# Late weights in small pieces that wait for attention products, a first projection by pieces, and a new instruction order

## The chip, the cores and the metric

The kernel runs on one core of one Trainium2 chip. The metric is the device time of one execution in microseconds (us); lower is better. Before the change it was 254.84 us (median of three runs, 253.96 to 255.41). A change under 2% counts as "same".

Four engines and a queue matter here: TensorE (PE; PEld is its weight load), VectorE (DVE), ScalarE (ACT), GpSimd (POOL), and SyncE (SP), which issues nearly all transfers, in order.

All runs told below are of the state called fast, but for one run of the kernel before (259.79 us), which the ratios leave out. Within that state, the mean clock that TensorE was granted still takes three values, about 1.0, 0.993 and 0.987, and that turns out to matter; it is given where it does.

## The reference

One block of a transformer with adaptive normalisation: modulation from a condition vector, attention over 8 dilated neighbours, and a gated feed-forward layer. S = 2048 rows (16 tiles of 128), D = 512, F = 1792 (14 hidden blocks of 128), 32 heads of 16.

```python
mod = (_silu(c) @ w_mod).reshape(1, 6, 1, -1)
sa, ca, ga, sb, cb, gb = ...                      # shift, scale, gate, twice
h = _layernorm(x) * (1 + ca) + sa
x = x + ga * _A_ref(h, A_wqkv, A_wo)              # attention: key and value rows s, s-2, ..., s-14
h = _layernorm(x) * (1 + cb) + sb
x = x + gb * _B_ref(h, B_w1, B_w3, B_w2)          # (silu(h @ w1) * (h @ w3)) @ w2
```

## The kernel before

The program is a list of operations with their dependences. A list scheduler, driven by a table of one number per operation, decides the order on each engine and which buffer each value gets; semaphore waits follow from that. So the table of numbers is part of the kernel.

The loads and what late loads wait for:

```python
LATE = {"wms1": 0, "wmg1": 2, "w13_0": 0, "w13_1": 1, "w13_2": 1, "w13_3": 2, "w2": 2}
...
p.dma(x_sb[:, 0:2, :], ...)                       # x of tiles 0, 1
p.dma(wm_s[0][:], wm_view[:, :, 0:1024], ...)     # shift and scale, 1 MB
p.dma(x_sb[:, 2:4, :], ...)
for i in range(3):                                # q, k, v thirds, 0.52 MB each
    p.dma(wqkv[:, :, i * D:(i + 1) * D], ...)
...
p.dma(wm_g[0][:], wm_view[:, :, 1024:1536], ...)  # first gate, 0.52 MB
...
for g in range(NG):                               # w1 and w3 by groups of hidden blocks
    late[f"w13_{g}"] = [p.dma(w1[:, :, a:b], ...), p.dma(w3[:, :, a:b], ...)]
late["w2"] = [p.dma(w2[:], w2_view, ...)]         # all of w2, 1.8 MB
...
for name, T in LATE.items():
    for o in late[name]:
        o.deps[prods[T]] = True                   # waits for attention product q*k of tile T
```

The table of numbers, and not this text, sets the order in which SyncE sends them: x of tiles 0 and 1, the first modulation's weights, x of tiles 2 and 3, the gate, x of tiles 12 to 15, v's and k's thirds, x of tiles 4 to 11, and q's third last.

The first h (normalised, modulated and transposed x of tiles 0 and 1) is written in four pieces by ScalarE and VectorE, and a projection product waits for all of it:

```python
def mm(e, ft=ft, vp=vp):
    for t in range(KT):
        ins = e.matmul(bank(vp)[:, 0:n], wqkv[:, t, col:col + P], vh.at[:, t, 0:n], start=(t == 0), stop=(t == KT - 1))
p.op("pe", mm, 4 * c_mm(n), k, r=[vh, vwq[kind]] + qkv_hold, w=[vp])
```

For each tile of rows VectorE makes one attention product q*k (`sb_pq`, 2.3 us) and one of attention by values (`sb_vsh`), and TensorE sums each with narrow products against 0/1 matrices. v goes out to memory and comes back shifted.

The last two tiles make their output in two halves of columns, each over all 14 hidden blocks at once:

```python
if T >= NT - 2:
    for q in range(2):
        def mm(e, q=q, vz=Val("ps_z", psum)):
            for fi in range(NF):
                ins = e.matmul(bank(vz)[:, 0:n], vhh[fi].at[:, tt * P:(tt + 1) * P], w2[:, fi, q * n:(q + 1) * n], ...)
        p.op("pe", mm, 7 * MM, ("z", 2 * T + q), r=vhh + [vw2s], w=[vz])
```

The softmax here doesn't subtract the row's maximum and nothing guards it: scores larger than these inputs give would overflow.

## Time and profile before

| | before |
|---|---|
| timed runs | 254.84 us median of 3 |
| span of the profiled execution | 253.0 us |
| TensorE / VectorE / ScalarE busy | 243.6 (96%) / 186.8 (74%) / 121.6 us (48%) |
| granted clock | 1.000 |

The prediction below shows the lines. In short: TensorE is full from 25 us to the end, so the kernel can only fill it earlier, take out the small stands in the full stretch, or end sooner.

How to read: in a timeline line the columns are start and length in us, engine, source line, operation, output from inputs, shapes and count; the bracket is the idle time just before it and what ended it. In a list of waits they are the engine and line that waited, what for, then us in total, times and longest. In a busy table each digit is the busy share of one fortieth of the span in tenths.

I also use one sum of my own, the *slip*: the start of a run of products on TensorE, less where it would start if the run before it took its count times the durations that the prediction derives (0.2158 us for 512 columns and so on). A slip is a stand, or a slow clock, or the drain of a pipeline.

### The profile page before, as it was taken

How to read it: one execution, taken by the hardware profiler on the slowest of the kernel's cores; microseconds unless marked ns; L12 is line 12 of the kernel's file. 1: busy time of each engine (PE TensorE's matmuls, PEld its weight loads, DVE VectorE, ACT ScalarE, POOL GpSimd, SP SyncE). 2: the span in 40 equal slices, each digit the busy share in tenths (PEclk: the TensorE clock that was granted, in tenths of full speed). 3: DMA queues.
4: the chain of work that ended last, by engine and by line, in shares of the span. 5: the costliest groups of instructions: out<-in, count | busy, mean ns of one | idle time of the engine just before them, and what ended most of it. 6: DMA issues, size and time to landing. Idle time of an engine off the chain costs nothing.

```text
span 253.0 us, 5719 instructions
## 1 busy us (share of the span) xinstructions
PE 243.6 (96%) x2413; PEld 146.9 (58%) x2413; DVE 186.8 (74%) x289; ACT 121.6 (48%) x214; POOL 18.5 (7%) x48
## 2 busy tenths in 40 slices
PE   7787999999999999999999999999999999999995
PEld 6666557665567766546655554455544444447774
DVE  4869599999998999999998898958714334623432
ACT  2376886845696357722561452333651332332320
POOL 4133100000000020000000200004100000100000
PEclk9999999999999999999999999999999999999999
DMA  6995999998598992270278373275122000021001
GB/s 228 354 327 155 288 336 252 341 323 213 139 254 207 295 273 66 57 173 25 89 190 231 55 208 64 42 191 143 26 60 83 1 3 0 0 62 44 21 3 41
DMA packets 48817, 37.09 MB, mean 147 GB/s; under 512 B 22152, under 2 KB 39576, under 8 KB 48792
## 3 DMA queue, kind: packets, MB, share of 16 engines
q1 hardware_dynamic: 48784, 36.73, 52.6%
q8 instruction: 19, 0.31, 0.5%
q14 instruction: 6, 0.05, 0.1%
q10 hardware_dynamic: 8, 0.00, 0.0%
HBM read 30.67 MB, written 5.26 MB: 142 GB/s over the span
## 4 chain that ended last, share of the span: by engine, by line
PE 85%; DMA 6%; SPq 4%; DVE 1%; ACT 1%; issue 0%; DVEq 0%
PE pall L847 36%; PE pall L883 17%; PE pall L691 9%; PE pall L831 5%; PE pall L818 5%; DMA sb_wqkv<-in_A_wqkv_dram 5%; PE pall L749 5%; SPq L135 4%; PE pall L709 4%; PE pall L870 2%; PE pall L650 2%; DMA sb_al<-a_scratch_dram 2%; DVE sb_vsh L809 1%; ACT sb_xn L611 1%; PE pall L535 0%
## 5 line engine op out<-in xcount | busy, mean ns | idle before, releaser
L847 PE MATMUL pall<-sb_h,sb_w 128*128 128x512 bf16 (+1 forms) x560 | 101.4, 336 | 0.0
L847 PEld LDWEIGHTS pall<-sb_h,sb_w 128*128 128x128 bf16 x560 | 53.6, 98 | 40.9 <-ACT sb_h L658 0.2
L853 ACT ACTIVATE sb_sg<-pall 128x512 bf16<-128x512 f32 (+1 forms) x70 | 35.3, 511 | 65.6 <-PE pall L847 65.6
L856 DVE TENSOR_TENSOR sb_hh<-sb_sg,pall 128x512 bf16<-128x512 bf16 (+1 forms) x70 | 38.8, 575 | 25.2 <-PE pall L847 24.6
L883 PE MATMUL pall<-sb_w,sb_hh 128*128 128x512 bf16 x196 | 43.9, 379 | 0.0
L740 DVE TENSOR_TENSOR sb_pq<-sb_q,sb_kT 128x4096 bf16<-128x4096 bf16 x16 | 36.2, 2284 | 3.6 <-ACT sb_q L698 3.2
L691 PE MATMUL pall<-sb_h,sb_wqkv 128*128 128x512 bf16 (+1 forms) x160 | 31.1, 336 | 2.5 <-DMA sb_wqkv<-in_A_wqkv_dram 2.5
L883 PEld LDWEIGHTS pall<-sb_w,sb_hh 128*128 128x128 bf16 x196 | 18.9, 98 | 21.8
L893 DVE TENSOR_TENSOR sb_o<-pall,sb_x 128x512 bf16<-128x512 f32 (+1 forms) x18 | 11.2, 629 | 22.7 <-PE pall L883 17.6
L592 DVE BATCH_NORM_STATS2 sb_st<-sb_x 128x6 f32<-128x512 bf16 x32 | 21.8, 681 | 4.6 <-DMA sb_x<-in_A_x_dram 4.3
L809 DVE TENSOR_TENSOR sb_vsh<-sb_vsh,sb_al 128x4096 bf16<-128x4096 bf16 x10 | 22.9, 2286 | 1.0 <-DMA sb_al<-a_scratch_dram 0.9
L691 PEld LDWEIGHTS pall<-sb_h,sb_wqkv 128*128 128x128 bf16 x160 | 14.6, 97 | 12.6 <-issue 2.0
L598 POOL TENSOR_TENSOR sb_rs<-sb_mv,sb_cst 128x2 f32<-128x2 f32 x16 | 5.3, 330 | 198.2 <-DVE sb_mv L593 151.9
L658 ACT ACTIVATE sb_h<-pall,sb_modc 128x512 bf16<-128x512 bf16 (+1 forms) x30 | 18.9, 707 | 1.7 <-PE pall L650 1.5
L611 ACT ACTIVATE sb_xn<-sb_x,sb_nb,sb_rs 128x512 bf16<-128x512 bf16 x16 | 12.1, 806 | 10.6 <-DVE sb_nb L605 10.5
L749 PEld LDWEIGHTS pall<-sb_E,sb_pq 128*128 128x128 bf16 x512 | 14.8, 96 | 3.2 <-DVE sb_pq L740 0.5
L709 PE MATMUL pall<-sb_wqkv,sb_h 128*128 128x512 bf16 x64 | 16.0, 378 | 0.3 <-DMA sb_wqkv<-in_A_wqkv_dram 0.3
L831 PE MATMUL pall<-sb_wo,sb_ot 128*128 128x512 bf16 x64 | 16.3, 379 | 0.0
L824 ACT ACTIVATE sb_ot<-pall 128x512 bf16<-128x512 f32 x16 | 9.5, 595 | 12.5 <-PE pall L818 12.5
L749 PE MATMUL pall<-sb_E,sb_pq 128*128 128x32 bf16 x512 | 15.1, 176 | 0.3 <-DVE sb_pq L740 0.3
L809 DVE TENSOR_TENSOR sb_vshx<-sb_vshx,sb_al 128x4096 bf16<-128x4096 bf16 x6 | 13.7, 2283 | 0.0
L698 ACT ACTIVATE sb_q<-pall 128x512 bf16<-128x512 f32 (+1 forms) x20 | 10.0, 517 | 5.8 <-PE pall L691 5.6
(70 smaller groups left out, 192.3 us busy)
## 6 DMA issues: line engine op xcount, KB each, us to landing
sb_vsh<-v_scratch_dram SPq DMA_DIRECT2D x40, 256.0 KB, 4.6
sb_vshx<-v_scratch_dram SPq DMA_DIRECT2D x24, 256.0 KB, 4.3
sb_wm_s<-in_w_mod_dram SPq DMA_DIRECT2D x2, 1024.0 KB, 6.4
v_scratch_dram<-sb_v SPq DMA_DIRECT2D x16, 128.0 KB, 3.9
sb_w<-in_B_w_dram SPq DMA_DIRECT2D x4, 512.0 KB, 4.6
sb_w<-in_B_w_dram SPq DMA_DIRECT2D x1, 1792.0 KB, 11.8
out_dram<-sb_o SPq DMA_DIRECT2D x14, 128.0 KB, 1.7
sb_x<-in_A_x_dram SPq DMA_DIRECT2D x3, 512.0 KB, 10.5
```

What stands on the lines that cost most here:

```text
L592: o = p.op("dve", lambda e, m=m, T=T: e.bn_stats(st[:, m, :], x_sb[:, T, :]), 670, ("st", m), r=[vx[T]], w=[vs])
L658: return e.activation(vh.at[:, ft, 0:n * P], b[:, j * 512:j * 512 + n * P], ACT.Identity, bias=modc[:, 8 * which + ft:8 * which + ft + 1], ...
L691: ins = e.matmul(bank(vp)[:, 0:n], wqkv[:, t, col:col + P], vh.at[:, t, 0:n], start=(t == 0), stop=(t == KT - 1))
L709: ins = e.matmul(bank(vp), vh.at[:, t, tt * P:(tt + 1) * P], wqkv[:, t, 2 * D:3 * D], start=(t == 0), stop=(t == KT - 1))
L740: return e.tensor_tensor(vp.at[:], in0, in1, ALU.mult)
L749: ins = e.matmul(b[:, c0:c0 + H], vp.at[:, w, ft, :], E_sb[:, ft, :], start=(ft == 0), stop=(ft == KT - 1))
L809: return e.tensor_tensor(v_w, v_w, a_w, ALU.mult)
L831: ins = e.matmul(bank(vy), vt.at[:, ft, :], wo[:, ft, :], start=(ft == 0), stop=(ft == KT - 1))
L847: ins = e.matmul(bank(vp)[:, 0:n], wt[:, t, fi * P:(fi + 1) * P], vh.at[:, t, 0:n], start=(t == 0), stop=(t == KT - 1))
L853: p.op("act", lambda e: e.activation(vt.at[:, 0:n], bank(vgp)[:, 0:n], ACT.Silu), c_act(n), k, r=[vgp], w=[vt], table="silu")
L856: p.op("dve", lambda e: e.tensor_tensor(vh_.at[:, 0:n], vt.at[:, 0:n], bank(vup)[:, 0:n], ALU.mult), c_dve(n), k, r=[vt, vup], w=[vh_])
L883: ins = e.matmul(bank(vz), vhh[fi].at[:, tt * P:(tt + 1) * P], w2[:, fi, :], start=(fi == 0), stop=(fi == NF - 1))
```

## The change

The intent: get the projections' weights in sooner by letting the gate wait; let the first q products start on the first piece of h; spread the late weights, in pieces, behind chosen attention products; end without waiting for the last hidden block; and find a new order for all of it by searching from many seeds. The diff, cut:

```diff
-LATE = {"wms1": 0, "wmg1": 2, "w13_0": 0, "w13_1": 1, "w13_2": 1, "w13_3": 2, "w2": 2}
+LATE = [("wmg0", -1), ("wms1", 1), ("wms1b", 2), ("wmg1", -1), ("w1_0", 3), ("w3_0", 12), ("w1_1", 3), ("w3_1", -1), ("w1_2",
+        0), ("w3_2", 5), ("w1_3", 5), ("w3_3", 4), ("w2_0", 4), ("w2_1", 8), ("w2_2", 0), ("w2_3", 16)]
...
-    late["wms1"] = [p.dma(wm_s[1][:], wm_view[:, :, 1536:2560], ("load", 12), 1048576, w=[vwms[1]])]
+    for name, a, i in (("wms1", 0, 12), ("wms1b", 512, 26)):
+        late[name] = p.dma(wm_s[1][:, :, a:a + 512], wm_view[:, :, 1536 + a:2048 + a], ("load", i), 524288, part=[vwms[1]])
...
-        late[f"w13_{g}"] = [
-            p.dma(w1[:, :, a:b], w1_view[:, :, a:b], ("load", 14 + g), 4 * 128 * (b - a) * 2, part=[vw13[g]]),
-            p.dma(w3[:, :, a:b], w3_view[:, :, a:b], ("load", 14 + g), 4 * 128 * (b - a) * 2, part=[vw13[g]]),
-        ]
+        late[f"w1_{g}"] = p.dma(w1[:, :, a:b], w1_view[:, :, a:b], ("load", 14 + 2 * g), 1024 * (b - a), w=[vw1[g]])
+        late[f"w3_{g}"] = p.dma(w3[:, :, a:b], w3_view[:, :, a:b], ("load", 15 + 2 * g), 1024 * (b - a), w=[vw3[g]])
...
-    late["w2"] = [p.dma(w2[:], w2_view, ("load", 18), 1835008, w=[vw2])]
+    for g in range(NG):
+        late[f"w2_{g}"] = p.dma(w2[:, a:b, :], w2_view[:, a:b, :], ("load", 22 + g), 131072 * (b - a), w=[vw2[g]])
...
+    ORDER = (2, 0, 3, 1)
+    def proj(mm, n, k, vh, vp, vw):          # the first h: one product per piece, each waits for its own
...
+        for t in ORDER:
+            o = p.op("pe", lambda e, t=t: mm(e, (t,)), c_mm(n), k, r=[vh.pieces[t], vw] + qkv_hold, part=[vp], hold=[vh],
+                     after=[o] if o else [])
...
-                p.op("pe", mm, 7 * MM, ("z", 2 * T + q), r=vhh + [vw2s], w=[vz])
+                for a, c in ((0, 10), (10, NF)):
...
+                    o = p.op("pe", mm, (c - a) * c_mm(n), ("z", 2 * T + q), r=vhh[a:c] + ..., part=[vz], after=[o] if o else [])
...
-    for name, T in LATE.items():
-        for o in late[name]:
-            o.deps[prods[T]] = True
+    for name, n in LATE:                     # even n: product q*k, odd n: attention by values, of tile n // 2
+        if n >= 0:
+            late[name].deps[(prods, avs)[n % 2][n // 2]] = True
...                                           # and the whole table of priorities is new
```

Also changed, and not shown: the modulation's result passes two VectorE operations instead of three, w2 is scaled in four pieces instead of two, and there are 104 warm-up products (products of ones that nobody reads) instead of 80.

## The prediction

> **What bounds the kernel now.** I read the busy shares first, then the 40 slices, then the chain that ended last for what one product of each shape costs, then PE's timeline where the slices are not full.
>
> ```profile
> span 253.0 us, 5719 instructions
> PE 243.6 (96%) x2413; PEld 146.9 (58%) x2413; DVE 186.8 (74%) x289; ACT 121.6 (48%) x214; POOL 18.5 (7%) x48
> ...
> PE   7787999999999999999999999999999999999995
> DVE  4869599999998999999998898958714334623432
> DMA  6995999998598992270278373275122000021001
> ```
>
> PE is full from the fifth slice (25 us) to the last. A change of order cannot shorten that stretch much; it can only make PE full earlier, or end it sooner. So I split the span into products that must be made and the rest. The chain gives start, length and count of back-to-back runs:
>
> ```profile
> 95.44 0.45 PE pall L650 x8
> 97.84 0.79 PE pall L749 x32
> 193.28 20.72 PE pall L847 x96
> 235.63 7.87 PE pall L847 x72
> ```
>
> One 512-column product takes 20.72/96 = 0.2158 us, one of 256 columns 7.87/72 = 0.1093, one of 16 or 32 columns 0.79/32 = 0.0247, a transpose 0.45/8 = 0.056. With the counts of the groups by shape: 756 of 512 columns, 163.1 us; 344 of 256, 37.6; 1024 of 16 or 32, 25.3; 104 transposes, 5.8; modulation and gates (96 one-column products and 8 spreads), about 2.8. Sum 234.6 us; the 80 warm-up products are not in it. From the last product to the end are 2.65 us (250.38 to 253.03). So 253.0 - 234.6 - 2.65 = 15.7 us are neither work nor end. The timeline of PE shows where:
>
> ```profile
> 6.83 0.94 PE L535 MATMUL pall<-sb_csT_bf,sb_wm_s 128*128 128x1 bf16 x32 [0.42 <-DMA sb_wm_s<-in_w_mod_dram]
> ...
> 8.98 0.55 PE L567 MATMUL pall<-sb_csT_bf,sb_wm_g 128*128 128x1 bf16 x16 [0.52 <-DMA sb_wm_g<-in_w_mod_dram]
> ...
> 12.09 1.02 PE L709 MATMUL pall<-sb_wqkv,sb_h 128*128 128x512 bf16 x4 [0.33 <-DMA sb_wqkv<-in_A_wqkv_dram]
> ...
> 14.87 2.36 PE L691 MATMUL pall<-sb_h,sb_wqkv 128*128 128x256 bf16 x20 [0.78 <-DMA sb_wqkv<-in_A_wqkv_dram]
> ...
> 21.14 1.91 PE L691 MATMUL pall<-sb_h,sb_wqkv 128*128 128x256 bf16 x16 [1.74 <-DMA sb_wqkv<-in_A_wqkv_dram]
> ...
> 72.60 0.96 PE L749 MATMUL pall<-sb_E,sb_pq 128*128 128x32 bf16 x32 [0.29 <-DVE sb_pq L740]
> ...
> 82.59 0.96 PE L818 MATMUL pall<-sb_ind,sb_vsh 128*128 128x16 bf16 x32 [0.23 <-DVE sb_vsh L809]
> ...
> 244.07 6.29 PE L870 MATMUL pall<-sb_w,sb_hh 128*128 128x256 bf16 x56 [0.59 <-DVE sb_hh L856]
> ```
>
> The three thirds of wqkv arrive one after another at 12, 15 and 21 us, and each time PE stands until then. By 21.14 us PE has done about 8.3 us of the work above, so 12.8 of the 15.7 us lie before. Laying the runs end to end at the durations above, starts slip behind by another 2.6 us after 26 us: 0.73 ahead of L870, and some 1.9 in small pieces, most at L749 and L818, which wait for VectorE's attention products between 50 and 90 us.
>
> VectorE is the second limit there: 9 tenths from 30 to 100 us. It gets its first attention product late:
>
> ```profile
> 28.58 2.29 DVE L740 TENSOR_TENSOR sb_pq<-sb_q,sb_kT 128x4096 bf16<-128x4096 bf16 x1 [3.15 <-ACT sb_q L698]
> ```
>
> It idled 3.15 us, because q needs the third of wqkv that lands at 21.
>
> **The Trainium skill.** "TensorE: Matmul & The Clock Gate", section "Back-to-back issue gap", gives N/2.4 + 2.5 ns for a warm product: 109.2 and 215.8 ns for 256 and 512 columns. The trace agrees (0.1093, 0.2158). The page's 131 ns for a sustained stream at 512 is not seen here, so nothing faster is to be hoped for. "Perfetto Trace Analysis", section "Identifying the Most-Contended Engine", says that matmul busy time is a poor measure; hence pitches and not the 96%. "DMA: Bandwidth & Descriptors", section "Where 436 GB/s comes from", puts memory's share of one core at about 358 GB/s; one-microsecond stretches of this trace move 345 to 355 GB/s from 7 to 17 us. So the head is bound by bytes, and the order of loads decides. The same page, "Queues, rings and completion order", says that each ring starts descriptors in order; the wqkv landings in order of issue agree.
>
> **The change part by part.** The lists of instructions of the two kernels show what moved; the products that must be made are the same, so the 234.6 us stay.
>
> *Head.* Before, the queue holds x of two tiles, the first half of modulation weights, x of two tiles, the gate's 0.52 MB, x, two thirds of wqkv, 1 MB of x, then the last third. After: x, modulation, wq, x, x, wk, wv, then 1 MB of x; the gate's weights come behind. Bytes issued ahead decide the landing, so I take it from the load in the same place before. wk closes 3.15 MB, where before the first wqkv third landed at 12.0; wv closes 3.67 MB, where the second landed at 14.85; wq closes 1.84 MB, between x of tiles 2 and 3 (7.44) and the gate's weights (8.96): 8.2. The first modulation still waits for its load until 6.83. Its result passes two VectorE operations of 0.15 us instead of three, and these no longer stand behind two statistics (they began at 9.09 and ended at 10.0; I get 8.0). The pieces of the first h come at 8.6 to 9.4, and since each product takes its own piece, the first q products run from 8.75. Then 24 warm-up products (1.3 us, harmless, as wk is not there), q and a first k, wk at 12.0 with 8 products to 12.95, transposes of h1 to 13.4 (its normalised tiles come at 12.9, after four statistics of 0.82 us that wait for x at 8.96 and 10.5), 4 products to 13.85, then a wait for wv to 14.95. From there the list runs on: 8 v (1.73), 8 k or q (0.87), 4 v (0.86), 12 more (1.31), 16 transposes (0.9), 19 products (2.08), 4 v (0.86): the first product on h2 at 23.6 us. Before, it began at 25.74 + 4 x 0.216 = 26.6, but with 0.6 us of gate and 0.22 of transposes done that now come later. Gain 26.6 - 23.6 - 0.8 = 2.2 us.
>
> *Middle.* The rest of PE's list sums to 221.7 us at these pitches, so its last product would end at 245.3. VectorE's first attention product moves to about 25.5 us; it then waits for the gate's product (PE's place 28.4, so to 29.5) and runs 1.3 us behind its own sum. Setting its sums against PE's, the attention products stand ready 0.65 to 1 us ahead of PE up to 55 us and 1.5 or more afterwards, where before they were level or up to 0.7 us late. So of the 1.9 us of small slips I expect 0.9 to stay; gain 1.0 with the 0.22 us of warm-up products that before stood at 70.5. The small pieces of w1, w3 and w2 total the same bytes; their waits spread them, and their reward is that the attention's round trip through memory meets fewer of them. w2's scaling, in four pieces instead of two, costs some 0.15 us more on VectorE, which has that much.
>
> *End.* The last two tiles' products take the first 10 hidden blocks, then the last 4, so nothing waits for the last block: the 0.59 us wait (0.73 with its drain) goes. The end after the last product stays 2.65 us.
>
> Sum: 2.2 + 1.0 + 0.7 = 3.9 us; the other way, 245.3 + 0.2 drain + 0.9 slips + 2.65 = 249.0. Span 249.1. The timed median is 1.8 us above the profiled span (254.84 against 253.0): 250.9, rounded to **250.8 us**, 1.6% faster.
>
> **The rivals.** *All waste goes:* if wv lands by bandwidth alone (3.67 MB/350 GB/s + 2.9 = 13.4) PE saves another 1 us, and with no slips 0.9 more: 248.9. For it: slack is everywhere positive. Against it: the second third of wqkv, in the same place, took until 14.85. *A new wait replaces the old one:* VectorE now has to make all 16 statistics before its first product, and a load that waits for an attention product blocks the in-order SyncE queue behind it, v and attention loads included. That would make PE stand for VectorE between 30 and 60 us: 252 to 254. For it: the ahead-times there are under 1 us; w3's second piece goes out before wo. Against: between 45 and 50 us, when the first attention rows return, few weights are in flight. *The head is hidden anyway*, PE running dry later and waiting for h3 and h4 until about 26: 253. Against: transposes of h3 are due only at 26 us, with their tiles made by 24.
>
> **Range and chances.** Errors: 1 us at wv's landing, 0.9 on slips, up to 2 to the bad side from the queue. Eight in ten: 249.0 to 252.8. Faster by 2% needs 249.74, 1.1 us better than my sum: 0.20. Slower by 2%: 0.01. Within: 0.79.
>
> **What would show it.** PE's first q product near 8.8 us, waits for wk to 12 and wv to 15, first 512-column product on h2 near 23.6; VectorE's first attention product near 25.5; no wait ahead of the last 256-column products; fewer and smaller waits at attention products. Wrong if wv lands two microseconds off, if PE shows waits for attention products of over 1 us in sum, or if a queue wait for a product delays a load PE then waits for.

## The result, and the profile after

Four runs of the changed kernel took 250.60 to 251.69 us, median 251.06; four of the kernel before, 253.96 to 255.41, median 254.54. The ratio is 0.9862, with a 95% interval of 0.9822 to 0.9902: 1.4% faster, "same" by the 2% line. (A ratio is the mean time of one kernel's fast runs over that of the other's of the same rounds, so it is not quite the ratio of the medians.) The spans of the two profiled executions are 253.0 and 248.6 us.

The head of the page after, with busy times and the busy table:

```profile
span 248.6 us, 5772 instructions
PE 243.5 (98%) x2437; PEld 149.2 (60%) x2437; DVE 186.8 (75%) x289; ACT 123.3 (50%) x216; POOL 21.3 (9%) x48
...
PE   8989999999999999999999999999999999999995
DVE  3869799999898999999899897898942344232442
DMA  6999969679979993336779270436032000001001
```

Busy times of TensorE and VectorE are what they were. The span is 4.4 us shorter: TensorE is full from the fourth slice (19 us) instead of the fifth (25 us). All of TensorE's waits that the trace after shows:

```profile
PE pall L702 <- DMA sb_wqkv<-in_A_wqkv_dram: 1.4, 1, 1.4
PE pall L551 <- DVE sb_ones L448: 1.1, 1, 1.1
```

Before there were nine such rows. The second is the wait for the first instruction of all, as before. The first is a wait for k's third of the projection weights. From TensorE's timeline after, the lines that answer to those of before:

```profile
7.00 0.94 PE L535 MATMUL pall<-sb_csT_bf,sb_wm_s 128*128 128x1 bf16 x32
...
8.77 0.75 PE L702 MATMUL pall<-sb_h,sb_wqkv 128*128 128x256 bf16 x3
...
13.55 1.03 PE L702 MATMUL pall<-sb_h,sb_wqkv 128*128 128x256 bf16 x8 [1.36 <-DMA sb_wqkv<-in_A_wqkv_dram]
...
15.30 1.89 PE L721 MATMUL pall<-sb_wqkv,sb_h 128*128 128x512 bf16 x8
...
23.91 2.75 PE L702 MATMUL pall<-sb_h,sb_wqkv 128*128 128x512 bf16 x12
...
239.75 6.28 PE L885 MATMUL pall<-sb_w,sb_hh 128*128 128x256 bf16 x56
```

The first q product starts at 8.77. k's third makes TensorE stand until 13.55; v's third makes it stand no more (no bracket at 15.30). The first 512-column product on the third h is at 23.91, against 26.6 before. The last products start with no bracket. VectorE's timeline after:

```profile
25.88 2.29 DVE L752 TENSOR_TENSOR sb_pq<-sb_q,sb_kT 128x4096 bf16<-128x4096 bf16 x1 [0.45 <-ACT sb_kT L711]
...
29.25 0.16 DVE L571 CAST sb_gcol<-pall 128x4 bf16<-128x4 f32 x1 [0.76 <-PE pall L565]
...
29.73 2.28 DVE L752 TENSOR_TENSOR sb_pq<-sb_q,sb_kT 128x4096 bf16<-128x4096 bf16 x1
```

The first attention product starts 2.7 us sooner than before (28.58), after an idle time of 0.45 instead of 3.15 us; then VectorE waits for the gate's product, which now comes late.

Summed over the trace, slips are 9.8 us before and 4.2 after; that is 5.6 us less for a span 4.4 us shorter, as the 24 more warm-up products take 1.3 us. After 26 us they fall from 2.6 us (of which 0.73 ahead of the last products) and 0.22 us of warm-up products to about 0.25.

### The profile page after: what moved, and what is told of

It reads as the page before. It is cut to its first block, busy times and chain, and to the rows that moved or that the text cites. A ratio compares the mean times of both kernels' runs of the same rounds, so it can differ in the third digit from the quotient of the medians.

```text
span 248.6 us, 5772 instructions
## 1 busy us (share of the span) xinstructions
PE 243.5 (98%) x2437; PEld 149.2 (60%) x2437; DVE 186.8 (75%) x289; ACT 123.3 (50%) x216; POOL 21.3 (9%) x48
## 4 chain that ended last, share of the span: by engine, by line
PE 94%; DMA 4%; SPq 1%; issue 0%; DVE 0%
PE pall L859 39%; PE pall L897 17%; PE pall L702 11%; PE pall L843 6%; PE pall L721 6%; PE pall L761 5%; PE pall L830 5%; DMA sb_wqkv<-in_A_wqkv_dram 4%; PE pall L885 2%; PE pall L649 2%; SPq L135 1%; PE pall L535 0%; PE pall L565 0%; PE pall L575 0%; DVE sb_o L907 0%
## 5 line engine op out<-in xcount | busy, mean ns | idle before, releaser
L897 PE MATMUL pall<-sb_w,sb_hh 128*128 128x512 bf16 x196 | 44.4, 379 | 0.0
L821 DVE TENSOR_TENSOR sb_vsh<-sb_vsh,sb_al 128x4096 bf16<-128x4096 bf16 x12 | 27.2, 2283 | 0.4 <-DMA sb_al<-a_scratch_dram 0.2
L843 PE MATMUL pall<-sb_wo,sb_ot 128*128 128x512 bf16 x64 | 15.8, 378 | 0.0
L598 POOL TENSOR_TENSOR sb_rs<-sb_rs,sb_cst 128x2 f32<-128x2 f32 x16 | 13.9, 871 | 1.3
```

Of the source, the lines that this page charges most:

```text
L821: return e.tensor_tensor(v_w, v_w, a_w, ALU.mult)
L843: ins = e.matmul(bank(vy), vt.at[:, ft, :], wo[:, ft, :], start=(ft == 0), stop=(ft == KT - 1))
L897: ins = e.matmul(bank(vz), vhh[fi].at[:, tt * P:(tt + 1) * P], w2[:, fi, :], start=(fi == 0), stop=(fi == NF - 1))
```

## The experiments

Twelve kernels ran, two of them controls, in three calls: the first two on chip 5, the third on chip 15. Edits to order were made on the finished lists of each engine, so that nothing else moved; `sp`, `dve`, `pe` and `pool` are those lists and `key(...)` finds an operation in them.

### The changed kernel again (two controls)

No edit.

> The changed kernel unaltered, as the control on this chip. Both theories: ratio to the kernel before 0.986, span near 248.6 us, TensorE without waits from 13.6 us on. It gives the spread against which the other three are read; a shift of under 0.3 us between two kernels of this call will count as nothing.

> Control: the changed kernel as it is, on the same chip and against the same runs of the kernel before: ratio 0.986, 250.6 to 251.3 us median, for comparison with the runs of this call. It also says how far two controls differ; I expect under 0.4 us.

The first gave 250.89 us median (ratio 0.9863, interval 0.9812 to 0.9913; before 255.34 without its slow run), the second 251.15 (0.9898, 0.985 to 0.9946; before 254.57). The gain is there on both chips. But the runs fall into two heaps: eight at a granted clock of 0.999 or 1.0 took 250.08 to 251.27, four at 0.992 or 0.993 took 253.32 to 253.90. I return to this below. So I also compare medians at like clock, that is among runs of one of these clocks alone; and as the eight alone range over 1.2 us, a difference of under about 1 us between medians is read below only where a trace shows its cause.

### The gate's load moved back ahead

```diff
+sp.remove(wmg0)
+sp.insert(sp.index(x23) + 1, wmg0)      # right behind x of tiles 2, 3, ahead of x of tiles 4-7, wk and wv
```

> The changed kernel with one transfer moved: the 0.52 MB of gate weights goes out directly after x of tiles 2 and 3, ahead of x of tiles 4 to 7 and of wk and wv, as in the kernel before. My theory (the head is bound by bytes, and TensorE is full ever after): wk and wv land 0.52 MB / 350 GB/s = 1.5 us later, TensorE waits for wk 1.3 to 1.5 us longer, and the end moves by 1.2 to 1.5 us (ratio about 0.991). Rival (the head is hidden; what counts is that VectorE starts its attention products early): the end moves by under 0.3 us.

254.35 us median, ratio 0.995 (0.9908 to 0.9992); 0.995 less 0.9863 of the control is 0.9% or 2.2 us slower, more than I expected. At like clock it is 2.9 us (253.52 against 250.67, clock about 1.0) or 0.7 (254.41 against 253.67, clock 0.993). TensorE's waits in its trace:

```profile
PE pall L535 <- DMA sb_wm_s<-in_w_mod_dram: 1.7, 1, 1.7
PE pall L702 <- DMA sb_wqkv<-in_A_wqkv_dram: 1.5, 1, 1.5
...
PE pall L830 <- DVE sb_vsh L821: 1.1, 1, 1.1
```

k's third now ends a wait at 15.34 us instead of 13.55. Part of that is not the edit: the first modulation's weights, which stand ahead of the gate in both, landed so late in this execution that their products began at 8.61 instead of 7.00. Other executions show the same lateness without the edit (8.96 in one below), so it varies by itself. With the edit, k's third is waited for longer although TensorE itself came later, and a new wait of 1.1 us for an attention product appears at 70.89 us. Ahead of that one VectorE itself stood, for rows of v on their way back from memory:

```profile
68.55 2.29 DVE L821 TENSOR_TENSOR sb_vsh<-sb_vsh,sb_al 128x4096 bf16<-128x4096 bf16 x1 [2.34 <-DMA sb_vsh<-v_scratch_dram]
```

So the gate's place in the queue is worth something between 0.7 and 2.9 us, about 2 over all runs; how much of that is the head and how much the later wait is not separated, as the late modulation is in the same trace.

### The kernel before, with only one load moved

q's third moved ahead of x of tiles 8 to 11 in the kernel before, which takes away the reason for the 1.74 us stand at 21 us.

```diff
+sp.remove(wq)
+sp.insert(sp.index(x8), wq)
```

> The kernel before with one transfer moved: the last third of wqkv (wq) goes out ahead of x of tiles 8 to 11 instead of behind it; nothing else changes. My theory (part of the gain is the place of wq alone): wq lands near 18 us instead of 21, TensorE's wait of 1.74 us ahead of 21.14 falls to under 0.3, VectorE's first attention product comes up to 1.7 us earlier, and the end moves forward by 1.3 to 1.7 us, so about 0.6% without any new order. Rival (TensorE's backlog or VectorE's late tiles take the gain back): under 0.5 us.

255.3 us, ratio 0.9999 (0.9962 to 1.0037): nothing. The theory that I had put down for this run fell. The stand at 21 us is gone, but these have come in its place:

```profile
PE pall L709 <- DMA sb_wqkv<-in_A_wqkv_dram: 1.6, 1, 1.6
PE pall L818 <- DVE sb_vshx L809: 1.2, 1, 1.2
PE pall L650 <- DVE sb_xn L615: 1.1, 1, 1.1
```

The first is not the edit's: it is for v's third, which stands ahead of the moved load and in this execution let its products begin 1.7 us later than in the first profile (13.82 against 12.09). The other two are places where time was given back. TensorE, done with its products more than a microsecond earlier, waits at 23 us for VectorE's normalised tile, because VectorE's list has a statistic of tiles 8 to 11 ahead of it, whose x the edit put behind q's third:

```profile
21.16 0.69 DVE L592 BATCH_NORM_STATS2 sb_st<-sb_x 128x6 f32<-128x512 bf16 x1 [2.03 <-DMA sb_x<-in_A_x_dram]
```

And it waits for an attention product at 90 us, ahead of which VectorE stood 1.52 us for rows of v. The order of VectorE's statistics and of the transposes has to follow the loads, or the time is given back. I take that to be what the new order does; no run shows it by itself.

### The first h as a whole

```diff
+for o in evictions_of_first_h: q.deps[o] = True          # first q product waits for all four pieces
+c = p.op("dve", lambda e: e.tensor_copy(p.modc[:, 0:8], p.modc[:, 0:8]), ...)   # a third operation on the modulation
```

> The changed kernel without two of its parts: the first q product waits for all four pieces of the first h, and a third VectorE operation on the modulation columns stands ahead of them, as in the kernel before. My theory: the first q products start some 0.8 to 1 us later, but they and the 28 warm-up products after them end before wk lands at 13.5, so the wait for wk shrinks by as much and the end moves by under 0.2 us. Rival (the early start is part of the gain): 0.7 to 1 us later.

251.25 us, ratio 0.9852 (0.9823 to 0.9882), by the ratio no different from the changed kernel; all its runs had a clock of 0.999 or 1.0, and the control's at that clock are 0.6 us below. The trace has a cause for that which is not the edit's, a wait of 0.8 us for the second modulation at 58 us, of which more below. At the head the first q product starts at 9.47 instead of 8.77 with a wait of 0.73 us, and the wait for k's third is 0.77 instead of 1.36: the one is paid out of the other, and the products behind k's third begin at 13.40 against 13.47 in the control. The piecewise first h is hidden behind k's landing and is worth nothing here.

### The last two tiles' products: undivided after, divided before

```diff
-for a, c in ((0, 10), (10, NF)):
+for a, c in ((0, NF),):
```

> The changed kernel with the last two tiles' products undivided, so that the first of them waits for all 14 hidden blocks; the lists of instructions are otherwise the same. My theory: a wait of about 0.6 us returns ahead of the last 56 products, and the end moves by 0.6 to 0.73 us. Rival (the new order already has the last block early enough): no wait, under 0.1 us.

251.61 us, ratio 0.987 (0.9832 to 0.9908). The trace shows the wait, and the slip with it is 0.74 us:

```profile
PE pall L885 <- DVE sb_hh L868: 0.6, 1, 0.6
```

All six of its runs had a clock of 0.999 or 1.0; their median is 0.9 us above that of the control's four runs at that clock (250.67, between 250.61 and 250.72). The ratios alone (0.987 and 0.9863) would not tell it from nothing, because two of the control's six runs had the lower clock. Nor do the 0.9 us show it by themselves: this trace too has a wait of 0.8 us for the second modulation, which the control's lacks. What shows it is the wait in the trace, with its slip. The reverse, the kernel before with the division alone:

> The kernel before with one part of the change alone: the last two tiles' products divided into 10 and 4 hidden blocks; all lists of instructions otherwise the same. My theory: the 0.59 us wait (0.73 with its drain) ahead of the last products goes and nothing else: 0.4 to 0.8 us faster than before, ratio about 0.997. Rival: the last hidden block is then needed at the fourth block of products anyway, or the extra wait costs as much: no difference.

254.84 us, ratio 1.0024 (0.9978 to 1.0069): no gain. The rival of the two was right. TensorE's timeline:

```profile
243.31 6.29 PE L872 MATMUL pall<-sb_w,sb_hh 128*128 128x256 bf16 x56 [0.58 <-DVE sb_hh L856]
```

The wait is still there, because in the list of the kernel before the last hidden block to be made is block 9, which belongs to the first ten. In the changed kernel it is block 11. The division pays only with an order that makes one of the last four blocks last.

### Late pieces without their waits

```diff
+for o in late: delete its dependence on an attention product      # same places in the queue
```

> The changed kernel with the pieces of w1, w3 and w2 in their places in SyncE's list, but without their waits for attention products. My theory (the list is in order, so the place decides and the wait adds little): the end moves by under 0.3 us either way. Rival (the waits hold transfers back from the attention's round trip through memory): VectorE waits for attention rows, and the end moves by 0.5 us or more.

251.55 us, ratio 0.9852 (0.9821 to 0.9884): by the ratio no change, as my theory had it. At like clock it is 0.9 us above the control (251.55 against 250.67), and its trace has a wait of 0.5 us for an attention product at 86.25, ahead of which VectorE stood 0.67 us for attention rows, as the rival had it; but this is also the execution in which the first modulation's products began at 8.96, after a wait of 1.9 us. So the waits named in the change's title are worth under about 1 us by themselves, and whether that is nothing these runs don't show. The trace shows why it is little: without the waits the first four pieces concerned leave at 34.4 us instead of 36.4, and all later ones within 0.7 us of where they left before. In an in-order queue the places of the pieces between v's and attention's transfers already spread them.

### All late pieces in one burst

```diff
+sp[i:] = late + rest        # about 5 MB of w1, w3 and w2 in one go, at about 31 us, without waits
```

> The changed kernel with all late pieces of w1, w3 and w2 (about 5 MB) sent in one burst from about 31 us, where the kernel before had them, without waits for attention products. My theory: 5 MB take about 14 us, so the first attention rows, written at 41 to 45 us and read back, come up to 1 to 2 us later; the lead of VectorE over TensorE is under 1 us there, so the end moves by 0.5 to 1.5 us. Rival (spreading the loads is worth nothing): under 0.3 us.

257.79 us, ratio 1.0105 (1.0074 to 1.0135): 6.9 us slower than the first control, far more than I had put down, and not by way of attention's rows. TensorE's waits and ScalarE's waits in its trace, one row of each:

```profile
PE pall L702 <- ACT sb_v L731: 4.4, 1, 4.4
```

```profile
ACT sb_v L731 <- DMA v_scratch_dram<-sb_v: 7.0, 1, 7.0
```

v has three buffers. Their write-outs stand in SyncE's queue behind the 5 MB, so no buffer comes free; ScalarE, which works in order, stands 7 us at the next eviction of v and with it holds up the evictions of q and k; then TensorE stands 4.4 us. The stretches of 2 us (the columns are the stretch, its length, then busy time and count for PE, PEld, DVE, ACT and POOL, the granted clock, the DMA share and GB/s) show a second price:

```profile
48.00:50.00 2.00, 0.00 (x0) 0.00 (x0) 0.00 (x0) 0.00 (x0) 0.00 (x0) 0.86 0.89 294
50.00:52.00 2.00, 1.00 (x3) 0.44 (x4) 0.05 (x1) 1.65 (x4) 0.00 (x0) 0.50 0.16 56
...
54.00:56.00 2.00, 2.00 (x6) 0.72 (x5) 2.00 (x2) 1.35 (x3) 0.00 (x0) 0.50 0.83 129
```

After the stand TensorE's clock is granted at half. It is busy all of 54 to 56 and makes six products. The slips are 4.59 us for the stand and 2.60 us for the slow stretch, 7.2 together, which is about the loss. "TensorE: Matmul & The Clock Gate", section "Part 1: The HAM clock gate", says that the clock falls to half when TensorE is idle for a window of about 3.4 us; adding up what is missing (0.14 x 2 + 0.5 x 6 + 0.07 x 2 over 48 to 58, the clock being 0.93 in the last stretch) gives 3.4 us lost, that is 6.8 us at half speed or two such windows.

### The same burst from another queue

```diff
+sp[:] = [o for o in sp if o not in late]
+for o in late: o.eng = "pool"           # the eleven transfers issued by GpSimd, from the same moment
+pool[i:i] = late
```

> The burst of the earlier run that cost 6.9 us (all late pieces of w1, w3 and w2 at about 31 us), but issued from GpSimd's queue instead of SyncE's; everything else the same. My theory: what cost the time was the line, v's write-outs standing behind 5 MB in the one in-order queue, so that v's three buffers were not freed and ScalarE stood at an eviction of v; with the burst in another queue the write-outs share the engines with it and most of the loss goes: 0 to 2.5 us above the control, and no wait of several us at ScalarE's evictions of v. Rival, it was the bytes in flight (any transfer in those 14 us is slow, whichever queue it stands in): 5 to 8 us above the control again, with the same TensorE wait of over 3 us near 51 us.

256.84 us, ratio 1.0092 (1.006 to 1.0124): 5.7 us above the control. By the total my theory fell and its rival stood; the trace shows that neither describes it. ScalarE's wait for v's write-out is gone from the list, as my theory had it, and so is the stand at 51 us. A different one takes its place. TensorE's, VectorE's and GpSimd's rows:

```profile
PE pall L649 <- DVE sb_xn L613: 4.8, 1, 4.8
```

```profile
DVE sb_xn L613 <- POOL sb_rs L598: 5.9, 1, 5.9
```

```profile
28.76 8.38 POOL L135 DMA_DIRECT2D sb_w<-in_B_w_dram  x11 [3.08 <-ACT sb_v L731]
```

Issuing eleven transfers takes GpSimd 8.38 us, 0.76 each, and the reciprocal root that the next normalised tiles need stands behind them on the same engine. TensorE's clock falls to half after this stand too (0.54 and 0.50 in the stretches from 36 to 42 us): the slips are 5.0 us for the stand and about 2 in the slow stretch. So the experiment did not isolate bytes from line. It speaks for the line in SyncE's queue as the cause of v's stand, without showing it, as the new stand of 5 us gave the write-outs time as well; and it shows that a line in GpSimd's queue costs nearly as much in another place.

### Two more products on VectorE

```diff
+for _ in range(2):
+    o = p.op("dve", lambda e: e.tensor_tensor(w1[:, :, 0:512], x[:, 0:4, :], x[:, 0:4, :], ALU.mult), ...)
+    dve.insert(dve.index(first), o)     # ahead of the second attention product; w1 is loaded over it later
```

> The changed kernel with two extra products of 128x2048 on VectorE (1.14 us each, 2.3 us) just before its second attention product. My theory (attention products stand ready 0.8 to 1 us ahead of TensorE there, and that lead is what removed the small waits of the kernel before): TensorE now waits for attention products 1.3 to 1.5 us in sum, and the end moves by as much, as TensorE never gets the time back. Rival A (VectorE is off the path): under 0.3 us. Rival B (VectorE is the bound from 26 us): 2.3 us.

254.2 us, ratio 0.9962 (0.9911 to 1.0013); the span is 2.4 us longer than the control's. TensorE's waits:

```profile
PE pall L761 <- DVE sb_pq L752: 1.5, 1, 1.5
...
PE pall L830 <- DVE sb_vsh L821: 0.5, 1, 0.5
PE pall L830 <- DVE sb_vshx L821: 0.4, 1, 0.4
```

The first came as expected: 2.4 us more work cost 1.5 us of wait, so VectorE had about 0.9 us in hand there. The other two I had not expected. They stand at 69 and 87 us, where I had thought that VectorE was 1.5 us ahead or more. VectorE's own waits ahead of the two products say what was late:

```profile
66.81 2.29 DVE L821 TENSOR_TENSOR sb_vsh<-sb_vsh,sb_al 128x4096 bf16<-128x4096 bf16 x1 [1.52 <-DMA sb_vsh<-v_scratch_dram]
...
85.08 2.29 DVE L821 TENSOR_TENSOR sb_vshx<-sb_vshx,sb_al 128x4096 bf16<-128x4096 bf16 x1 [0.88 <-DMA sb_al<-a_scratch_dram]
```

VectorE was idle there and not behind with work: it stood for rows of v and of attention that come back from memory (from 62 to 70 us the DMA engines are busy throughout, share 1.06 to 1.09). In the first profile of the changed kernel the waits for such rows are 0.21 and 0.23 us. So what is close behind TensorE between 60 and 90 us is the trip through memory; whatever delays it, here VectorE's later products, comes out as a wait for VectorE.

### A version meant to beat both

```diff
+sp: wk ahead of x of tiles 4-7
+pe: 24 warm-up products removed; q2's rest and k1 ahead of h1's transposes; h2's transposes after q6, k7, q2, q5
+dve: tiles 2, 3 normalised before the statistics of tile 4 on; tiles 4-7 before those of tile 12 on
```

> A candidate to beat both: the changed kernel with the second third of the projection weights (wk) loaded ahead of x of tiles 4 to 7, 24 warm-up products taken out of TensorE's list, and the q and k products, statistics and transposes of the first tiles moved up to fit. My theory: wk, landing about 1.4 us earlier, removes the 1.36 us wait for it, but VectorE's lead over TensorE at the attention products is only 0.3 to 1 us at several places (two extra products on VectorE cost 2.4 us of span), so of what the head gives at most the lead can be kept: median 0.2 to 0.8 us below the control of the same call. Rival, VectorE is the true bound: x of tiles 4 to 7 lands later, VectorE has no earlier first attention product, and the median is level with the control or up to 1 us above it, with new waits for sb_pq or sb_vsh.

252.62 us, ratio 0.992 (0.9873 to 0.9968); the control gave 0.9898. Its three runs at a clock of 1.0 took 250.93, 251.34 and 252.14 us, the control's four 250.62 to 251.27: no gain. The rival was right about the time, but its sign, new waits for attention products, did not come. TensorE's timeline:

```profile
24.40 1.90 PE L702 MATMUL pall<-sb_h,sb_wqkv 128*128 128x512 bf16 x8 [1.13 <-ACT sb_h L657]
...
59.80 0.95 PE L535 MATMUL pall<-sb_csT_bf,sb_wm_s 128*128 128x1 bf16 x32 [1.62 <-DMA sb_wm_s<-in_w_mod_dram]
```

The wait for k's third is gone; TensorE waits 0.8 us for v's third instead, and at 24.40 for the third h, whose normalised tiles VectorE now makes later (its first attention product is at 26.58, 0.7 us later than in the changed kernel). In this execution the first modulation was 1 us late as well, so not all of that is the edit.

The second line shows something else. The second modulation's weights, which before the change were issued at 31.9 us and used at 46.9, are now in two pieces that wait for attention products; the later one leaves at about 52 us and its products are due at 57.5. In the changed kernel's first profile there is no wait; in its second control 0.33 us; in the runs with the first h as a whole and with the undivided products 0.8, and no slow clock after it; here 1.62. And after it, in stretches of 1 us:

```profile
61.00:62.00 1.00, 1.00 (x5) 0.40 (x4) 1.00 (x1) 0.32 (x1) 1.00 (x1) 0.86 0.98 245
62.00:63.00 1.00, 1.00 (x4) 0.36 (x3) 1.00 (x4) 0.28 (x1) 0.92 (x2) 0.50 1.08 243
...
65.00:66.00 1.00, 1.00 (x6) 0.46 (x5) 0.00 (x0) 0.52 (x2) 0.00 (x0) 0.93 1.11 306
```

One window at half speed, 0.14 + 3 x 0.5 + 0.07 = 1.7 us lost, right after a stand of 1.6. The mean clock of this execution is 0.993, which is what one such window makes of it (1.7/252.6 = 0.007). The slips are 1.77 and 1.69 us.

## Why the prediction was right, and where it was not

The time was 251.06 us against 250.8 predicted, inside the range, and the class was right. By its own steps:

**What bounds the kernel.** Right. TensorE's work did not change, and the gain came from waste: slips 9.8 to 4.2 us. VectorE as "the second limit there" holds at the first attention products; between 60 and 90 us the runs that add work or delay show VectorE itself waiting for rows from memory (1.52 and 2.34 us).

**Head, 2.2 us.** It came to 26.6 - 23.91 - 0.8 = 1.9 us, but not by the steps as put. "wk at 12.0" was wrong: it took until 13.55, and the wait there was 1.36 us. "Then a wait for wv to 14.95" was wrong as well: v's products started at 15.30 without waiting. The two errors cancelled by luck, as TensorE was later and the last third's landing was not. The step that failed is reading a landing from the bytes in the same place of one execution: k's third, waited for in the first profile and the first control, was not waited for in the second control, which waited 0.8 us for v's third at 14.80 instead. The landing itself varies by over a microsecond. That the pieces of the first h start q early is right (8.77 against 8.75 put down) and worth nothing (the whole-h run). That the gate's load is what had to get out of the way is supported by its run, about 2 us. That "the head is bound by bytes" agrees with the 345 to 355 GB/s that the prediction read from 7 to 17 us; but from 4 to 7 us the same trace moves 395, 401 and 379 GB/s, so the 358 that it names is no fixed ceiling.

**Middle, 1.0 us.** Mis-sized: 1.9 us with the warm-ups. "So of the 1.9 us of small slips I expect 0.9 to stay" was the term; 0.25 stayed in the first profile, and 0.5 and 0.8 in those of the two controls. The lead that I worked out of 0.65 to 1 us was real at the first place, and enough to close nearly all slips. Where the prediction said "1.5 or more afterwards", the run with two more products says less: TensorE waits at 69 and 87 us when VectorE is put 2.4 us back, and what was late there was the rows and not VectorE's sum. "Their waits spread them, and their reward" was half wrong: taking the waits away changes less than about 1 us, while one burst costs 6.9 us, and by v's write-outs and a half-speed clock rather than by attention's round trip. How much of the 1.9 us the new order brought and how much the spread of the pieces I did not separate.

**End, 0.7 us.** Right in size: 0.73 us of slip gone, 0.74 back when the division is undone. What I did not say is that the division needs the order: alone in the kernel before it gives nothing.

**From span to time.** The spans differ by 4.4 us, by 0.5 more than the sum of 3.9, yet the medians by 3.5. The term "timed median is 1.8 us above the profiled span" is where they part: the profiled execution before was timed at 255.0 us, above its median, and the one after at 250.6, below its own; in both the time is 2.0 us above the span. (The sum gave 250.9, which was put down as 250.8.) That the time came within 0.3 us is so in part luck: the span fell 0.5 us below the 249.1 put down, and the other runs lay above the profiled one.

**The rivals.** "All waste goes" (248.9) did not happen; 4.2 us of slips are left, nearly all before 14 us. "A new wait replaces the old" did not show in the changed kernel's profile, but its edge does: rows from memory between 60 and 90 us, and the second modulation's late load, for which TensorE waits a little or not at all when all is well. "Head hidden" (253) fell.

**What stays open.** Four of the twelve control runs had a clock of 0.992 or 0.993 and took about 3 us longer than the others. The version above shows one way to that, a late second modulation of 1.6 us and a half-speed window of 1.7, and the sum (3.3) is near, but no profile fell in a slow-clock run of the changed kernel itself, so that this is their cause is argued, not shown. In the kernel before runs at 0.993 are not slower than those at 1.0 (median 254.5 against 255.3 for the runs beside the experiments); in two profiled variants of it the half-speed window lies at 8 to 12 and at 10 to 14 us, where TensorE waits for loads anyway. So the gain depends on the clock: between the controls and the kernel before at about 1.0 it is 4.7 us on chip 5 and 3.6 on chip 15, but under 1 us on both between runs at 0.993 (253.7 against 254.4, and 253.6 against 254.5). A kernel with the second modulation's load issued some microseconds sooner is what I would try next; it was not run.

## What to carry to other kernels

When an engine is full, look for the gain where it is not yet full, and expect loads and order to pay only together: the load moved alone and the division alone each gave nothing, because the wait moved to the next thing that was late or stayed where it was. When an engine seems late, look at what it waited for itself: VectorE's late products were late rows. Put little in the way of what an engine needs first, let what can wait stand behind it, and before making transfers wait or putting many in one line, ask which write-outs stand behind them and which buffers those hold. A stand of TensorE can cost twice, once as a stand and once as the slow clock after it, so compare runs by granted clock, and by the waits that vary from execution to execution, before believing a difference of one per cent.

## What the Trainium skill lacked or had wrong

- "TensorE: Matmul & The Clock Gate", "Part 1: The HAM clock gate": the length of the half-speed window agrees (3.4 us, from 1.7 us lost). The page has an idle window of about 3.4 us as its cause; here a stand of 1.62 us, followed by 0.95 us of one-column products, was enough in one execution, while a stand of 1.5 us in the middle of the run with two more products was not (clock 1.0), nor were two stands of 0.8 us at the same place. Which windows fall could not be told from the page for these stands.
- The same page, "Back-to-back issue gap", gives 131 ns for a sustained stream of 512-column products; the traces here show 215.8 at full clock, which is what its formula for a warm product gives.
- "DMA: Bandwidth & Descriptors" has no figure for how much the same load's landing varies between executions: the first modulation's products began between 6.83 and 8.96 us, and the wait for k's third went from 1.4 us to none with the queue unchanged.
- I found no page with the time that GpSimd is held to issue a transfer of 0.4 or 0.5 MB: 8.38 us for eleven here, 0.76 each, in which other work of that engine stands. It belongs to "DMA: Bandwidth & Descriptors".
